# The copies out of the product with v: ScalarE's and VectorE's declared free of each other

## The chip, the cores and the metric

One core of one Trainium2 chip runs the whole kernel. The metric is the device time of one launch in microseconds (us). Below, TensorE is PE in the profile, VectorE DVE, ScalarE ACT, GpSimd POOL, and SyncE (which issues nearly all DMAs) SP.

## The reference

Attention with a threshold feeds a bilinear feed-forward layer. All data are float32.

```
q, k, v: (8 batches, 8 heads, 576 positions, 64)
s    = q @ k.T / 8                                   # 576 x 576 per head
s    = where(s >= max(s) - tau, s, -1e9)             # per row
w    = exp(s - max(s)); w = w / (sum(w) + 1e-9)
attn = w @ v
x    = attn as (8*576, 8*64) = (4608, 512)
out  = ((x @ w_a) * (x @ w_b)) @ w_out               # d_ff = 1536
```

## The kernel before

The work of the attention is cut into units. A unit is one pair of heads of one batch (32 pairs in all, `pairs`) and 128 queries; u = 4 is the remaining 64 queries of the pair. The main loop runs over the units, g counts them. One turn of it does, for unit g:

- `scores` (L335 on): TensorE multiplies q with k into two PSUM tiles `sc`, one for each head (matmuls of L347). VectorE takes the row maxima `mx` (L354) and subtracts tau, `thr` (L355).
- `weigh`: ScalarE makes the bias (L374) and the exponential `tw` (L375); VectorE compares with the threshold, multiplies and sums (L378, one operation for each head; with it the PSUM tile `sc` becomes free).
- `reciprocal` (L387 or L389, then L391 on VectorE) and `normalise` (L397 on ScalarE).
- one turn later `turn_blocks`: VectorE transposes blocks (L441), SyncE's DMAs write them to DRAM (L452) and, another turn later, read them back turned (L461, `wT`).
- three turns later (`PV_LAG`) `weighted`: the product with v. `product` fills one PSUM tile `pv` (L478), and `settle` copies it out.

`settle` is the place of the change. `pv` covers two PSUM banks, `pv[:, 0]` and `pv[:, 1]`. ScalarE copies the first bank to the left half of the target's columns (L485, `out[:, 0:n]`). VectorE copies the second bank to the right half in two operations, since its upper and lower 64 partitions trade places (L487). The target is `xT` (256 positions of a batch) or, for the last 64 positions, `xt`. When the last third of a pair's queries is done, `weighted` calls `settle` twice on the same `pv`: first columns 0 to 128 into `xT`, then 128 to 160 into `xt` (28 times in the run). The four products of the first batch's tails have `xt` alone.

The layer that records the program orders every pair of operations that touch the same tiles. So in the kernel before VectorE's copies of a `settle` wait for ScalarE's copy, and in the double call ScalarE's copy into `xt` waits for VectorE's copies into `xT`, and VectorE's copies into `xt` for that.

The first eight units (`BY_PE`) go another way: their weights are turned by TensorE (`turn_pe`, L422, copied out by ScalarE in L424 and by VectorE in L425), and `weighted_unit` calls `settle` once for each with 64 columns. In this stretch the weights of the feed-forward layer are converted too (L242, L243 on ScalarE, L249 and L268 on GpSimd, L255 and L263 on VectorE).

The feed-forward layer is a generator, `ffn`, that `advance` moves on by a number of matmul columns at several points of each turn, so that TensorE has work between the attention's steps. It multiplies the blocks `xT` and `xS` (the same with its halves of partitions exchanged, made by GpSimd in L495) with w_a and w_b into PSUM tiles `pab` (L683, and L622 in `seven_of`, which uses a scheme with seven products instead of eight), and the product of both with w_out into `po` (L728). Its PSUM tiles are emptied by ScalarE (L689, L629, L467) and VectorE (L691, L631, L638, L640, L645, L468).

All PSUM tiles (`tp`, `sc`, `pv`, `pab`, `po`) come from one pool of four slots of two banks each. A slot is given on when the last reader of its tile is done. At the end `keep_order` fixes the order of instructions on each engine as written; an engine works through its list in that order.

Of the kernel before, what the change touches and what calls it, by code (L numbers as in the profile page):

```python
# [52 lines left out]
def kernel(  # L53
# [38 lines left out]
    nc = tc.nc  # L92
    B, H, S, D = q.shape
    P = 128
# [6 lines left out]
    TAIL = S - MAIN  # L101
# [7 lines left out]
    GT = HALF // TAIL  # L109
# [16 lines left out]
    def banks(n, name):  # L126

        return psum.tile([P, 2, 512], FP32, tag="banks", name=name)[:, :, 0:n]
# [147 lines left out]
    for _ in range(TW_BUFS):  # L276
        t = work.tile([P, 2 * NB, Q], FP32, tag="tw", bufs=TW_BUFS, name="rows")
# [31 lines left out]
    x_of, xtail_of = {}, {}  # L309
# [123 lines left out]
    def width(i, h):  # L433
        return (HALF, HALF, TAIL)[h] if i < HP else (HALF, HALF + TAIL)[h]
# [35 lines left out]
    def product(wT, vm, n):  # L470

        pv = banks(n // 2, "pv")
        for s in range(NSLOT):
            for j in range(2):
                rows = slice(j * D, (j + 1) * D)
                for c in range(2):
                    y = j ^ c
                    nc.tensor.matmul(pv[c * D:(c + 1) * D, y], vm[rows, s], wT[y](rows, s),  # L478
                                     start=(s == 0), stop=(s == NSLOT - 1))
        return pv  # L480

    def settle(out, pv, c0, c1):

        n = c1 - c0
        nc.scalar.copy(out[:, 0:n], pv[:, 0, c0:c1])  # L485
        for c in range(2):
            nc.vector.tensor_copy(out[c * D:(c + 1) * D, n:2 * n], pv[(1 - c) * D:(2 - c) * D, 1, c0:c1])  # L487

    def x_tile(name):
        return work.tile([P, HP, HALF], FP32, tag="xT", bufs=XT_BUFS, name=name)  # L490

    def exchange(x, xs, hp, c0, c1, engine):

        for r in range(2):
            engine.tensor_copy(xs[r * D:(r + 1) * D, hp, c0:c1], x[(1 - r) * D:(2 - r) * D, hp, c0:c1])  # L495
# [17 lines left out]
    def weighted_unit(i, u):  # L513

        b, hp = pairs[i]
        wT = turned.pop((i, u, "pe"))
        pv = product([lambda rows, s, t=t: t[rows, s] for t in wT], loaded[i]["v"], P)
        if (b, 0) not in x_of:
            x_of[b, 0] = x_tile("xT")
            state["xs"] = x_tile("xS")  # L520
        settle(x_of[b, 0][:, hp, u * P:(u + 1) * P], pv, 0, D)
        exchange(x_of[b, 0], state["xs"], hp, u * P, (u + 1) * P, nc.gpsimd)
        if hp == HP - 1:
            state["rows"] = u + 1
            if u == 0:
                blocks.append(((x_of[b, 0], state["xs"]), ("first", b, 0)))

    def weighted(i, h):

        b, hp = pairs[i]  # L530
        n = width(i, h)
        if h < 2:
            groups = G + (n > HALF)
            wT = [turned.pop((i, 2 * h + y))[:, 0:groups] for y in range(2)]
        else:
            t = turned.pop((i, NT))
            wT = [t[:, y:y + 1] for y in range(2)]
        pv = product([lambda rows, s, t=t: t[rows, :, s] for t in wT], loaded[i]["v"], n)
        if h < 2:
            if hp == 0:  # L540
                x_of[b, h] = x_tile("xT")
            settle(x_of[b, h][:, hp, :], pv, 0, P)
            if hp == HP - 1:
                complete.append((x_of.pop((b, h)), ("half", b, h)))
        if n % HALF:
            t = b % GT
            if hp == 0 and t == 0:
                xtail_of[b // GT] = x_tile("xt")
            settle(xtail_of[b // GT][:, hp, t * TAIL:(t + 1) * TAIL], pv, (n - TAIL) // 2, n // 2)
            del loaded[i], prepared[i]  # L550
            if hp == HP - 1 and t == GT - 1:
                complete.append((xtail_of.pop(b // GT), ("tail", b - t, 0)))
# [319 lines left out]
    n = 0  # L872
# [4 lines left out]
    for g in range(len(units) + PV_LAG):  # L877
# [4 lines left out]
        if here:  # L882
            i, u = units[g]
# [6 lines left out]
        if 2 <= g < BY_PE + 2:  # L890
            weighted_unit(*units[g - 2])
            running["owed"] -= NSLOT * P // 2
# [23 lines left out]
        if g > BY_PE:  # L916
            advance(PORTIONS[1] * pace)
            n = g - PV_LAG
            if BY_PE <= n < len(units) and part(*units[n]):
                make_room()  # L920
                weighted(*part(*units[n]))
                running["owed"] -= NSLOT * width(*part(*units[n])) // 2
            if BY_PE + 1 < g <= len(units) + 1:
                turn_back(*units[g - 2])
# [78 lines left out]
```

## Time and profile before

| what | value |
|---|---|
| median of 3 runs | 1473.59 us (1470.5 to 1475.08) |
| the profiled execution's own time | 1469.17 us |
| its span in the profile | 1467.4 us |
| granted TensorE clock, mean | 0.996 |
| TensorE busy | 1404.0 us (96% of the span) |
| VectorE busy | 1020.5 us (70%) |
| ScalarE busy | 678.8 us (46%) |
| GpSimd busy | 490.4 us (33%) |
| copies of L485 (ScalarE) | 100: 68 into xT, 32 into xt |
| copies of L487 (VectorE) | 200: 136 into xT, 64 into xt |
| a copy of L485, 128x128 and 128x32 | 0.267 us and 0.186 us |
| a copy of L487, 64x128 and 64x32 | 0.285 us and 0.188 us |

A line of the waits reads: who waited <- what ended the wait: total us, how often, longest. A line of the timeline reads: start, us, engine, source line, operation, what it writes<-what it reads, how often merged into this line, and in square brackets the idle time of the engine just before and what ended it. The times are those of one execution. A matmul's end is modelled, not recorded.

### The profile page before, as it was taken

The page shows a single profiled execution, that of the slowest core. Times are in us where ns is not written, and L with a number is a line of the kernel's source. Part 1 is how long each engine was busy: PE and PEld are TensorE (multiplying, and loading weights), DVE is VectorE, ACT ScalarE, POOL GpSimd, SP SyncE. Part 2 cuts the span into 40 slices and gives each one's busy share as a digit, 9 for nine tenths or more (in the row PEclk, how much of TensorE's full clock was granted, in tenths as well). Part 3 has the DMA queues.
Part 4 walks back from the last instruction along what each step waited for, and adds up shares of the span by engine and source line. Part 5 has one row for each costly group of instructions (what it writes and reads, how often), then busy time and mean ns, then how long its engine had stood idle before and what let it go on. Part 6 is the DMA issues. An engine that isn't in the chain of part 4 may idle for free.

```text
span 1467.4 us, 70219 instructions
## 1 busy us (share of the span) xinstructions
PE 1404.0 (96%) x31136; PEld 1224.5 (83%) x31136; DVE 1020.5 (70%) x2295; ACT 678.8 (46%) x1259; POOL 490.4 (33%) x678
## 2 busy tenths in 40 slices
PE   5779999999999999999999999999999999999998
PEld 4667687788978788899889978789898879989998
DVE  6888687778776877776757777677767786644314
ACT  5877455445544554544444545344544454331011
POOL 2764703333161606042425233241516060605000
PEclk9999999999999999999999999999999999999999
DMA  9977677678656775767545866377746776450000
GB/s 206 217 198 209 159 178 193 170 165 205 176 142 160 183 199 139 178 158 174 138 129 126 193 166 162 101 165 187 184 126 153 173 180 169 120 138 17 3 17 17
DMA packets 325056, 222.82 MB, mean 152 GB/s; under 512 B 169616, under 2 KB 308880, under 8 KB 324752
## 3 DMA queue, kind: packets, MB, share of 16 engines
q1 hardware_dynamic: 322384, 217.73, 60.1%
q8 instruction: 245, 4.01, 1.2%
q10 hardware_dynamic: 2368, 0.59, 0.2%
q14 instruction: 59, 0.48, 0.1%
HBM read 128.58 MB, written 89.65 MB: 149 GB/s over the span
## 4 chain that ended last, share of the span: by engine, by line
PE 81%; DVE 9%; DMA 4%; issue 2%; ACT 2%; SPq 1%; POOL 1%; DVEq 0%; ACTq 0%
PE pab L683 33%; PE po L728 18%; PE pab L622 11%; PE pv L478 9%; PE sc L347 9%; DVE mx L354 2%; DMA wT<-swap 2%; DVE tw L441 1%; DVE tw L378 1%; SPq L452 1%; PE po L774 1%; DVE low L255 1%; DVE xT L487 0%; POOL h L697 0%; POOL xU L502 0%
## 5 line engine op out<-in xcount | busy, mean ns | idle before, releaser
L397 ACT ACTIVATE tw<-tw,rcp 128x576 f32<-128x576 f32 x272 | 197.8, 769 | 221.9 <-DVE rcp L391 221.9
L354 DVE TENSOR_REDUCE mx<-sc 128x1 f32<-128x576 f32 x288 | 205.2, 749 | 106.2 <-PE sc L347 104.5
L375 ACT ACTIVATE tw<-sc,bias,scalars 128x576 f32<-128x576 f32 x288 | 239.7, 832 | 9.9 <-ACT bias L374 0.2
L378 DVE SCALAR_TENSOR_TENSOR tw<-sc,thr,tw 128x576 f32<-128x576 f32 x288 | 224.2, 800 | 14.1 <-ACT tw L375 13.0
L728 PE MATMUL po<-wo_sb,h 64*64 64x256 f32 x3264 | 217.0, 377 | 5.3 <-DVE t L640 5.2
L588 POOL TENSOR_TENSOR t<-u,t 128x512 f32<-128x512 f32 x14 | 17.8, 1275 | 542.1 <-ACT t L629 502.0
L441 DVE STREAM_TRANSPOSE tw<-tw 128x576 f32<-128x576 f32 x272 | 196.0, 754 | 0.8 <-ACT tw L397 0.8
L347 PE MATMUL sc<-kT,qT 64*64 64x288 f32 x2016 | 188.1, 404 | 2.4 <-DVE tw L378 1.5
L478 PE MATMUL pv<-wT,vm 64*64 64x160 f32 (+3 forms) x5184 | 183.6, 273 | 6.4 <-DMA wT<-swap 3.5
L728 PEld LDWEIGHTS po<-wo_sb,h 64*64 64x64 f32 x3264 | 159.1, 133 | 34.8 <-DVE t L640 6.4
L683 PE MATMUL pab<-xS,wa_sb 64*64 64x256 f32 (+1 forms) x2560 | 177.3, 366 | 1.8 <-issue 1.8
L478 PEld LDWEIGHTS pv<-wT,vm 64*64 64x64 f32 x5184 | 164.7, 134 | 17.0 <-issue 7.3
L683 PE MATMUL pab<-xS,wb_sb 64*64 64x256 f32 (+1 forms) x2560 | 176.2, 366 | 0.9 <-issue 0.9
L697 POOL TENSOR_TENSOR h<-h 128x256 f32<-128x256 f32 x168 | 117.7, 736 | 165.7 <-PE po L728 162.2
L683 PE MATMUL pab<-xT,wa_sb 64*64 64x256 f32 (+1 forms) x2304 | 156.1, 366 | 6.1 <-ACT wo_sb L242 1.8
L728 PE MATMUL po<-sums_u,h 64*64 64x256 f32 x2448 | 158.5, 376 | 0.6 <-DVE h L645 0.6
L683 PE MATMUL pab<-xT,wb_sb 64*64 64x256 f32 (+1 forms) x2304 | 156.9, 365 | 1.6 <-DVE h L691 1.0
L683 PEld LDWEIGHTS pab<-xS,wa_sb 64*64 64x64 f32 x2560 | 130.5, 133 | 18.9 <-issue 2.2
L683 PEld LDWEIGHTS pab<-xS,wb_sb 64*64 64x64 f32 x2560 | 131.1, 133 | 16.5 <-issue 1.6
L728 PEld LDWEIGHTS po<-sums_u,h 64*64 64x64 f32 x2448 | 118.2, 133 | 22.8 <-DVE h L645 1.0
L347 PEld LDWEIGHTS sc<-kT,qT 64*64 64x64 f32 x2016 | 111.2, 133 | 28.7 <-issue 6.3
L683 PEld LDWEIGHTS pab<-xT,wa_sb 64*64 64x64 f32 x2304 | 114.8, 134 | 22.1 <-ACT wo_sb L242 2.0
(119 smaller groups left out, 2003.8 us busy)
## 6 DMA issues: line engine op xcount, KB each, us to landing
swap<-tw SPq DMA_DIRECT2D x480, 144.0 KB, 2.6
wT<-swap SPq DMA_DIRECT2D x120, 576.0 KB, 4.5
vm<-in_v_dram SPq DMA_DIRECT2D x128, 72.0 KB, 3.1
swap<-tw SPq DMA_DIRECT2D x128, 72.0 KB, 1.8
kT<-in_k_dram SPq DMA_DIRECT2D x112, 72.0 KB, 4.3
wT<-swap SPq DMA_DIRECT2D x56, 144.0 KB, 2.6
out_dram<-kept SPq DMA_DIRECT2D x30, 256.0 KB, 4.0
raw<-in_moe_w_a_dram SPq DMA_DIRECT2D x18, 256.0 KB, 6.6
```

The lines of the kernel that those rows point to most:

```text
L347: nc.tensor.matmul(sc[j if u < NT else 0][to, c], qT[r, q0:q0 + D], kT[r, c * SH:(c + 1) * SH], start=True, stop=True)
L354: nc.vector.tensor_reduce(mx[:, c], sc[j], axis=AX.XY, op=ALU.max)
L375: nc.scalar.activation(wb[j], sb[j], AF.Exp, bias=bias[:, j:j + 1], scale=e_scale)
L378: nc.vector.scalar_tensor_tensor(out=wv, in0=sb[j], scalar=thr[:, j:j + 1], in1=wv, op0=ALU.is_ge, op1=ALU.mult, accum_out=sums[:, j:j + 1])
L397: nc.scalar.activation(w, w, AF.Copy, scale=rcp[:, j:j + 1])
L441: nc.vector.transpose(w, w)
L478: nc.tensor.matmul(pv[c * D:(c + 1) * D, y], vm[rows, s], wT[y](rows, s), start=(s == 0), stop=(s == NSLOT - 1))
L588: (nc.vector if state["over"] else nc.gpsimd).tensor_tensor(*a, **kw)
L622: nc.tensor.matmul(pab[c * D:(c + 1) * D, r, y * P:(y + 1) * P], w[k][rows, w0:w0 + D], moving[k][rows], start=(k == 0), stop=(k == HP - 1))
L683: nc.tensor.matmul(pab[c * D:(c + 1) * D, r], w[rows, f // n, k, fs + c * D:fs + (c + 1) * D], moving, start=(k == 0), stop=(k == H - 1))
L697: (nc.vector if state["over"] else nc.gpsimd).tensor_tensor(*a, **kw)
L728: nc.tensor.matmul(po[c * D:(c + 1) * D, r, y], ht[rows, t0:t0 + D], other[rows, f], start=(f == 0), stop=(f == NF // 2 - 1))
```

## The change

`settle` gets the list of the copies made so far from the same `pv`, by engine. Every copy of ScalarE is declared independent of every copy of VectorE, of the same call and of an earlier call on the same `pv`. No instruction is added, removed or moved in its engine's list; only what they wait for changes, and with it which of the four PSUM slots some tiles are given.

```
-    def settle(out, pv, c0, c1):
+    def settle(out, pv, c0, c1, others):

         n = c1 - c0
-        nc.scalar.copy(out[:, 0:n], pv[:, 0, c0:c1])
-        for c in range(2):
-            nc.vector.tensor_copy(out[c * D:(c + 1) * D, n:2 * n], pv[(1 - c) * D:(2 - c) * D, 1, c0:c1])
+        one = [nc.scalar.copy(out[:, 0:n], pv[:, 0, c0:c1])]
+        two = [nc.vector.tensor_copy(out[c * D:(c + 1) * D, n:2 * n], pv[(1 - c) * D:(2 - c) * D, 1, c0:c1])
+               for c in range(2)]
+        for mine, theirs in ((one, others[1] + two), (two, others[0] + one)):
+            for a in mine:
+                for b in theirs:
+                    tc.declare_no_dep(a.ins, b.ins, reason="banks of their own")
+        others[0].extend(one)
+        others[1].extend(two)
...
-        settle(x_of[b, 0][:, hp, u * P:(u + 1) * P], pv, 0, D)
+        settle(x_of[b, 0][:, hp, u * P:(u + 1) * P], pv, 0, D, ([], []))
...
+        read = [], []
         if h < 2:
             if hp == 0:
                 x_of[b, h] = x_tile("xT")
-            settle(x_of[b, h][:, hp, :], pv, 0, P)
+            settle(x_of[b, h][:, hp, :], pv, 0, P, read)
...
-            settle(xtail_of[b // GT][:, hp, t * TAIL:(t + 1) * TAIL], pv, (n - TAIL) // 2, n // 2)
+            settle(xtail_of[b // GT][:, hp, t * TAIL:(t + 1) * TAIL], pv, (n - TAIL) // 2, n // 2, read)
```

## The prediction

> **What bounds the kernel now.** I read the page's busy times and chain first, then the waits of TensorE, then those of VectorE and ScalarE, then the timeline around single settles. The page:
>
> ```profile
> PE 1404.0 (96%) x31136; PEld 1224.5 (83%) x31136; DVE 1020.5 (70%) x2295; ACT 678.8 (46%) x1259; POOL 490.4 (33%) x678
> ...
> PE 81%; DVE 9%; DMA 4%; issue 2%; ACT 2%; SPq 1%; POOL 1%; DVEq 0%; ACTq 0%
> ```
>
> TensorE is the bound. What VectorE saves counts only where TensorE waits for it. The second line, the chain that ended last, says that 9% of the span runs through VectorE, and the chain in order of time shows most of it before 125 us, where weights are converted. The waits of TensorE between 125 and 1330 us (who <- for whom: us in total, times, longest):
>
> ```profile
> PE po L728 <- DVE t L640: 5.2, 5, 1.7
> PE pv L478 <- DMA wT<-swap: 3.5, 3, 2.2
> PE pab L622 <- DVE h L691: 2.7, 3, 1.2
> PE sc L347 <- DVE tw L378: 2.3, 2, 1.5
> ...
> PE pab L622 <- DVE u L631: 1.8, 2, 1.1
> ```
>
> All rows of this view come to 22.9 us, of which VectorE's are 14.9 us in 16 waits. That is the stock from which the change can draw. The waits it aims at stand in the waits of all engines:
>
> ```profile
> DVE xT L487 <- ACT xT L485: 127.8, 58, 6.3
> ...
> ACT xt L485 <- DVE xT L487: 18.4, 28, 0.7
> ...
> DVE xt L487 <- ACT xt L485: 8.2, 30, 0.9
> ```
>
> The first row is no gain of 127.8 us: ScalarE had itself waited for the product with v (183.4 us in 65 waits), so most of it is the wait for TensorE, only put down to the copy that came last. The timeline of one double settle shows what is the copies' own:
>
> ```profile
> 323.35 0.27 ACT L485 COPY xT<-pv 128x128 f32<-128x128 f32 x1 [1.88 <-PE pv L478]
> ...
> 323.65 0.59 DVE L487 COPY xT<-pv 64x128 f32<-64x128 f32 x2 [1.46 <-ACT xT L485]
> ...
> 324.27 0.19 ACT L485 COPY xt<-pv 128x32 f32<-128x32 f32 x1 [0.66 <-DVE xT L487]
> ...
> 324.49 0.39 DVE L487 COPY xt<-pv 64x32 f32<-64x32 f32 x2 [0.25 <-ACT xt L485]
> ...
> 325.18 1.40 DVE L354 TENSOR_REDUCE mx<-sc 128x1 f32<-128x576 f32 x2
> ...
> 328.71 0.67 PE L347 MATMUL sc<-kT,qT 64*64 64x288 f32 x5 [1.45 <-DVE tw L378]
> ```
>
> ScalarE starts when pv is done, VectorE only 0.30 us later, 0.03 us after ScalarE's end; the tail is a third and fourth link. VectorE then has no idle time until L378, for which TensorE waits 1.45 us.
>
> **What the Trainium skill says.** "Trainium Architecture — The Big Picture", section Inside one NeuronCore: the engines have their own instruction streams and meet only through semaphores; so a dropped dependency lets both copies start at once. The trace agrees insofar as each copy starts some 0.03 us after the one it waited for. "PSUM — Partial Sum Buffer", section Specifications (TRN2): ScalarE and VectorE can read PSUM in parallel at full bandwidth if they don't collide in a bank. The copies use a bank each. The trace has no settle in which both copies run, but VectorE's L354 reads PSUM as fast beside ScalarE's PSUM reads as without (timeline: two take 1.41 us at 42.32 beside L485 and L375, 1.40 us at 325.18 beside neither). "VectorE: DVE Perf Modes", section The DRAIN you can't avoid: a semaphore between operations costs VectorE nothing extra; so I give the shed signals themselves no price. No run here isolates that. "SBUF — State Buffer", section Who interferes with whom: VectorE and GpSimd take a shared port by an exclusive lock. The trace agrees: `thr` (L355) takes 0.23 us alone and 0.5 to 0.6 us beside GpSimd.
>
> **The change, part by part.** Compared as built, both programs have the same instructions in the same order on all five engines; only waits and PSUM slots differ.
>
> *A single settle into xT (L487 no longer waits for L485).* VectorE starts with ScalarE: 0.267 us for the copy plus 0.03 us, 0.30 us earlier. This holds for the single settles after 125 us, but for three (185, 193 and 1200 us) where VectorE is late anyhow.
>
> *A double settle.* VectorE gains 0.30 us, and the 0.25 us gap before xt goes too: 0.55 us, 28 times. ScalarE's 0.66 us gap goes, so its L397 is bound by VectorE's reciprocal alone, and moves up by the same 0.55 us.
>
> *The first eight settles (29 to 90 us).* Here nothing is won:
>
> ```profile
> 50.82 0.60 DVE L355 TENSOR_SCALAR thr<-mx,scalars 128x2 f32<-128x2 f32 x1
> ...
> 51.24 0.20 ACT L485 COPY xT<-pv 128x64 f32<-128x64 f32 x1
> ...
> 51.47 0.46 DVE L487 COPY xT<-pv 64x64 f32<-64x64 f32 x2
> ```
>
> VectorE comes from L355 0.03 to 0.05 us before its copy; ScalarE's copy is over by then in all eight. Cost 0.
>
> *PSUM slots.* The pool now sees pv's slot come free by two engines, and in units 4 to 9 two tiles swap slots six times. Later tiles have the same predecessors under other slot names. The one swap that can hurt is the second sc of unit 4 (near 40.5 us): it takes the slot that VectorE's second L378 frees at 40.7 us instead of one that ScalarE's L424 freed at 40.2 us. That is 0.2 us of TensorE at most. VectorE doesn't read that tile before 42.3 us, so it is hidden; were VectorE not behind there, it would cost the 0.2 us.
>
> *Added waits.* TensorE waits for two engines instead of one at pv's slot, VectorE's L255 also for ScalarE. Each new one is for a copy that ends no later than the one formerly last. Bounds: 0, and 0.05 us (a semaphore instruction on TensorE's queue lasts 0.051 us) times the three that are new: 0.15 us. I take 0.
>
> *What reaches TensorE.* VectorE's 0.55 or 0.30 us dies in its first idle time afterwards (mostly 'mx L354 <- PE sc L347': 95.3 us in 66 waits). So I went through the stretches in which TensorE lost over 0.15 us, and asked whether VectorE sat idle between the last settle and the instruction that released TensorE. I measured the loss between starts, because a matmul of 256 columns is issued every 0.054 us but shown 0.377 us long, so that the idle figure hides up to 0.3 us. After double settles, without idle time between, TensorE loses 0.38 us at 286.8, 0.93 at 305.7, 1.64 at 328.7, 0.56 at 480.7, 0.67 at 505.0, 1.30 at 932.9, 1.39 at 1007.2, 1.22 at 1099.9 and 0.42 at 1170.0 (there by ScalarE, itself behind the reciprocal). Each shrinks by the smaller of loss and 0.55: 0.38 + 7 x 0.55 + 0.42 = 4.65 us. At 631.3 it waits 0.19 us for pv's own slot, which goes. At 715.0 and 854.7, after single settles with 0.09 us idle between, 2 x 0.21 = 0.42. Sum 5.2 us.
>
> What is not won: at 942.8 (1.74 us for L640), 386.9 and 272.1 VectorE idled 1.5 us or more in between; the DMA waits for wT hang on L441, which follows such an idle time. What is late next where a stall goes: the same VectorE operation, since seven of the nine losses are above or near 0.55 us; at 286.8, 480.7 and 1170.0 it is TensorE itself. A gain of TensorE stays: all later units hang on TensorE, and the tail from 1330 us is TensorE without a wait.
>
> So the profiled execution goes from 1469.17 to 1464.0 us (1.8 us around the span stay). It lies 4.4 us under the median of the runs, below even the fastest; I take the same difference from the median: 1473.6 - 5.2 = 1468.4 us.
>
> **The rivals.**
>
> *Hidden anyway.* TensorE's waits aren't VectorE's alone: with it 0.55 us earlier, a transfer, ScalarE or the next full slot holds TensorE. For it: 96% busy, and the gaps are nine in 1200 us. Against it: in the timelines of the nine the releaser ran without idle time. If half or more is absorbed, 0 to 2.6 us are won: about 1472.3 us.
>
> *A cascade.* ScalarE and VectorE free pab and po slots earlier in stalls that the view gives to "issue", and L441's DMAs go out earlier, so that waits for wT shrink too. All of VectorE's 14.9 us can't go; doubling my gain is the limit that I see: 1463 us.
>
> *Slower: the copies hurt each other.* Place: the 60 settles into xT after 125 us, where both copies would start together. If each VectorE copy grows by over 0.15 us (half of 0.30), the pair ends later than before. Doubled to 0.57 and 0.38 us, a double settle ends 0.57 + 0.38 - 0.55 = 0.40 us later; at the nine places and some four single ones that is 9 x 0.40 + 4 x 0.27 = 4.7 us: 1478 us. Against it: the L354 row above, and ScalarE's L375 with 0.83 us throughout, whatever VectorE reads.
>
> *It does nothing* can be left out: the built program waits for PE at L487.
>
> **How the numbers follow.** Forecast 0.56, hidden 0.33, cascade 0.05, slower 0.06. A measurement of this kernel tells about 0.3% (4.4 us) from no change. The forecast's own range is 3.5 to 7 us of gain, 1466.6 to 1470.1, and 0.46 of its 0.56 lie beyond 4.4 us; with the cascade, faster 0.51. Same: 0.10 + 0.33 = 0.43, and slower 0.06. VectorE's port lock with GpSimd shifts with every change of timing: L355 differs by 0.3 us a time, at nine places, either sign, about 1 us. The range reaches from 1464.5, most of the cascade left out, to 1474.0, no gain at all with a little of that.
>
> **What would show it.** The waits of L487 for L485 must be gone, L487 waiting for pv in L478 instead, and starting within 0.1 us of L485; the gap before ScalarE's xt copy too. L487 stays at 0.285 and 0.188 us; longer ones speak for the collision. TensorE's waits for VectorE after 125 us fall from 14.9 to about 10 us, most of all at L640, L378 and L631. VectorE's idle time before L354 grows. Wrong would be: those waits gone but TensorE's unchanged (hidden), or the same sum under DMA or ScalarE.

## The result and the profile after

| what | before | after |
|---|---|---|
| median of the runs | 1472.87 us (1470.5 to 1476.39, 6 runs) | 1464.95 us (1462.41 to 1467.27, 6 runs) |
| ratio, 95% interval | | 0.9944 (0.9926 to 0.9961) |
| the profiled execution's own time | 1469.17 us | 1465.3 us |
| its span | 1467.4 us | 1463.5 us |

By the ratio the change makes the kernel faster by 0.56%, 8.2 us, with 5.7 to 10.9 us inside the interval (the two medians differ by 7.9 us). The forecast was 1468.4 us; the time lies in its range, 0.45 us above the lower end. The gain is larger than the 5.2 us of the sum, which lies outside the interval, and larger than the 3.9 us by which the two profiled executions differ. TensorE's granted clock is no cause of it: its mean over the runs is 0.9960 with the change (6 runs), 0.9955 in the 35 runs of the kernel before that stand beside the first experiments, and 0.9953 in the 6 runs of the second kernel below, which has the whole gain. So two questions are open: where the rest of the gain comes from, and why the two profiles show only half of it.

In the changed file the lines after the edit have moved: ScalarE's copies are still L485, VectorE's are now L486; L622, L631, L640, L645, L683, L691, L697 and L728 are now L629, L638, L647, L652, L690, L698, L704 and L735. First the page of the changed kernel, busy times and the chain that ended last:

```profile
PE 1401.9 (96%) x31136; PEld 1209.2 (83%) x31136; DVE 1021.0 (70%) x2295; ACT 676.8 (46%) x1259; POOL 490.8 (34%) x678
...
PE 80%; DVE 8%; DMA 6%; SPq 2%; issue 2%; ACT 2%; DVEq 0%; ACTq 0%
```

No engine works less: VectorE has 1021.0 us as before it had 1020.5. What moved is when it works. The waits of all engines in the changed kernel (who <- for whom: us in total, times, longest):

```profile
ACT tw L397 <- DVE rcp L391: 218.4, 149, 4.6
...
DVE xT L486 <- PE pv L478: 117.6, 57, 6.0
DVE mx L354 <- PE sc L347: 113.8, 81, 3.8
```

The three waits of the copies for one another are gone; VectorE now waits for TensorE's pv itself. The timeline of the settle that the prediction showed at 323.35 us:

```profile
321.65 0.27 ACT L485 COPY xT<-pv 128x128 f32<-128x128 f32 x1 [1.89 <-PE pv L478]
321.65 0.59 DVE L486 COPY xT<-pv 64x128 f32<-64x128 f32 x2 [1.17 <-PE pv L478]
321.81 0.19 ACT L485 COPY xt<-pv 128x32 f32<-128x32 f32 x1
...
322.25 0.39 DVE L486 COPY xt<-pv 64x32 f32<-64x32 f32 x2
...
322.94 1.40 DVE L354 TENSOR_REDUCE mx<-sc 128x1 f32<-128x576 f32 x2
...
326.32 0.95 PE L347 MATMUL sc<-kT,qT 64*64 64x288 f32 x11 [0.76 <-DVE tw L378]
```

Both copies start together and last as long as before (0.27, 0.19, 0.59 and 0.39 us), so from pv's end to L354 there are 1.29 us instead of 1.83: 0.54 us less. TensorE's wait for L378 shrinks from 1.45 to 0.76 us. TensorE's waits between 125 and 1330 us, after:

```profile
PE pv L478 <- DMA wT<-swap: 6.6, 6, 2.0
PE po L735 <- DVE t L647: 4.4, 4, 1.7
PE pab L629 <- DVE h L698: 2.2, 3, 1.2
...
PE sc L347 <- DVE tw L378: 1.5, 2, 0.8
PE pab L629 <- DVE u L638: 1.4, 2, 0.8
```

VectorE's rows come to 11.0 us in 14 waits, from 14.9 in 16. But the first row grew from 3.5 to 6.6 us: this execution happened to wait longer for transfers. To see both apart I compared how far TensorE had come: both traces have all 31,136 matmuls, so I took for each unit the median start of its score matmuls (L347) in one trace and in the other, and from unit to unit what TensorE won or lost. This gives 160 steps for each pair of traces. A unit's matmuls are spread over some microseconds, so with another of them in place of the median a gain can move to the step before or after, and single figures by some 0.1 us.

### The profile page after: what moved, and what is told of

It is laid out like the page before. It is cut to its first block, busy times and chain, and to the rows that moved or that the text cites. A ratio compares the mean times of both kernels' runs of the same rounds, so it can differ in the third digit from the quotient of the medians.

```text
span 1463.5 us, 70223 instructions
## 1 busy us (share of the span) xinstructions
PE 1401.9 (96%) x31136; PEld 1209.2 (83%) x31136; DVE 1021.0 (70%) x2295; ACT 676.8 (46%) x1259; POOL 490.8 (34%) x678
## 4 chain that ended last, share of the span: by engine, by line
PE 80%; DVE 8%; DMA 6%; SPq 2%; issue 2%; ACT 2%; DVEq 0%; ACTq 0%
PE pab L690 30%; PE po L735 18%; PE pab L629 12%; PE pv L478 10%; PE sc L347 9%; DMA wT<-swap 4%; DVE mx L354 2%; DVE tw L441 1%; SPq L452 1%; DVE tw L378 1%; DMA kT<-in_k_dram 1%; PE po L781 1%; DMA vm<-in_v_dram 1%; DVE low L255 1%; DVE thr L355 0%
## 5 line engine op out<-in xcount | busy, mean ns | idle before, releaser
L397 ACT ACTIVATE tw<-tw,rcp 128x576 f32<-128x576 f32 x272 | 197.8, 769 | 218.4 <-DVE rcp L391 218.4
L354 DVE TENSOR_REDUCE mx<-sc 128x1 f32<-128x576 f32 x288 | 205.4, 750 | 114.9 <-PE sc L347 113.8
L378 DVE SCALAR_TENSOR_TENSOR tw<-sc,thr,tw 128x576 f32<-128x576 f32 x288 | 224.1, 800 | 14.6 <-ACT tw L375 13.7
L735 PE MATMUL po<-wo_sb,h 64*64 64x256 f32 x3264 | 218.6, 377 | 4.7 <-DVE t L647 4.4
L347 PE MATMUL sc<-kT,qT 64*64 64x288 f32 x2016 | 189.3, 403 | 1.7 <-DVE tw L378 0.8
L735 PEld LDWEIGHTS po<-wo_sb,h 64*64 64x64 f32 x3264 | 159.8, 133 | 34.5 <-DVE t L647 5.3
L690 PE MATMUL pab<-xS,wa_sb 64*64 64x256 f32 (+1 forms) x2560 | 178.0, 366 | 2.3 <-issue 2.3
L690 PE MATMUL pab<-xS,wb_sb 64*64 64x256 f32 (+1 forms) x2560 | 176.8, 366 | 0.9 <-issue 0.9
L704 POOL TENSOR_TENSOR h<-h 128x256 f32<-128x256 f32 x168 | 117.7, 736 | 167.1 <-PE po L735 163.8
L690 PE MATMUL pab<-xT,wa_sb 64*64 64x256 f32 (+1 forms) x2304 | 156.3, 365 | 5.5 <-DVE tw L378 2.9
L735 PE MATMUL po<-sums_u,h 64*64 64x256 f32 x2448 | 160.0, 376 | 0.0
L690 PE MATMUL pab<-xT,wb_sb 64*64 64x256 f32 (+1 forms) x2304 | 157.9, 365 | 1.3 <-DVE h L698 1.1
L690 PEld LDWEIGHTS pab<-xS,wa_sb 64*64 64x64 f32 x2560 | 128.7, 133 | 22.1 <-issue 2.7
L690 PEld LDWEIGHTS pab<-xS,wb_sb 64*64 64x64 f32 x2560 | 128.7, 133 | 19.7 <-issue 1.5
L735 PEld LDWEIGHTS po<-sums_u,h 64*64 64x64 f32 x2448 | 118.6, 133 | 22.8 <-DVE h L652 0.3
L347 PEld LDWEIGHTS sc<-kT,qT 64*64 64x64 f32 x2016 | 113.1, 133 | 26.8 <-issue 3.3
L690 PEld LDWEIGHTS pab<-xT,wa_sb 64*64 64x64 f32 x2304 | 112.7, 133 | 23.7 <-POOL xS L501 3.3
```

The costliest lines, as they stand in the source:

```text
L347: nc.tensor.matmul(sc[j if u < NT else 0][to, c], qT[r, q0:q0 + D], kT[r, c * SH:(c + 1) * SH], start=True, stop=True)
L354: nc.vector.tensor_reduce(mx[:, c], sc[j], axis=AX.XY, op=ALU.max)
L378: nc.vector.scalar_tensor_tensor(out=wv, in0=sb[j], scalar=thr[:, j:j + 1], in1=wv, op0=ALU.is_ge, op1=ALU.mult, accum_out=sums[:, j:j + 1])
L397: nc.scalar.activation(w, w, AF.Copy, scale=rcp[:, j:j + 1])
L690: nc.tensor.matmul(pab[c * D:(c + 1) * D, r], w[rows, f // n, k, fs + c * D:fs + (c + 1) * D], moving, start=(k == 0), stop=(k == H - 1))
L704: (nc.vector if state["over"] else nc.gpsimd).tensor_tensor(*a, **kw)
```

## The experiments

Four kernels were run beside the kernel before on one chip (its median there: 1470.86 us in 35 runs).

**Only the first eight settles freed.** Only the calls of `weighted_unit` declare the copies independent. This kernel has all the swaps of PSUM slots that the change brought.

```
-    def settle(out, pv, c0, c1, others):
+    def settle(out, pv, c0, c1, others=None):
...
+        if others is None:
+            return
         for mine, theirs in ((one, others[1] + two), (two, others[0] + one)):
...
-            settle(x_of[b, h][:, hp, :], pv, 0, P, read)
+            settle(x_of[b, h][:, hp, :], pv, 0, P)
...
-            settle(xtail_of[b // GT][:, hp, t * TAIL:(t + 1) * TAIL], pv, (n - TAIL) // 2, n // 2, read)
+            settle(xtail_of[b // GT][:, hp, t * TAIL:(t + 1) * TAIL], pv, (n - TAIL) // 2, n // 2)
```

> Only the first eight settles (64 columns) are freed; from unit 8 on the copies stay ordered as before. The six swaps of PSUM slots in units 4 to 9 come with it. Theory A (VectorE starts 0.30 or 0.55 us earlier in the later settles, and that shows where TensorE waits for VectorE): ratio to before 0.999 to 1.001, since in the first eight VectorE comes late to its copies anyway. Theory B (the start and the other PSUM slots brought the gain): ratio about 0.9945, as the whole change.

Measured: 1470.93 us, ratio 0.9996 (0.9986 to 1.0006). The start and the slots bring nothing that the interval of 1.5 us either way would show. The timeline of the changed kernel says why, as it did before:

```profile
50.86 0.61 DVE L355 TENSOR_SCALAR thr<-mx,scalars 128x2 f32<-128x2 f32 x1
...
51.33 0.18 ACT L485 COPY xT<-pv 128x64 f32<-128x64 f32 x1
51.50 0.46 DVE L486 COPY xT<-pv 64x64 f32<-64x64 f32 x2
```

VectorE still comes from L355 at 51.47 us, when ScalarE's copy is nearly over.

**Only the later settles freed.** The opposite half: `settle` as above, but only `weighted_unit` leaves the list out.

```
-        settle(x_of[b, 0][:, hp, u * P:(u + 1) * P], pv, 0, D, ([], []))
+        settle(x_of[b, 0][:, hp, u * P:(u + 1) * P], pv, 0, D)
```

> Only the settles from unit 8 on are freed; the first eight stay ordered, and no PSUM slot differs from before. Theory A: the whole gain, ratio 0.993 to 0.9965 (1462 to 1468 us). Theory B: ratio 0.999 to 1.0.

Measured: 1463.56 us, ratio 0.9945 (0.9927 to 0.9963). The whole gain is here.

**Free, but VectorE later.** The changed kernel; VectorE makes one of its two copies twice, so that it ends about as late as if it had waited.

```
-               for c in range(2)]
+               for c in (0, 1, 0)]
```

> All copies are free of each other as in the change, but VectorE repeats one of its two copies in every settle (0.285 us into xT, 0.188 us into xt), so that its queue is as late behind a settle as before: 0.285 against 0.30 us after a single one, 0.47 against 0.55 us after a double one; ScalarE stays free. Theory A (it is VectorE's time): back to before, ratio 0.998 to 1.0005. Theory C (it is the wait itself: the signal's handling, or ScalarE freed of its 0.66 us gap): the gain stays, ratio 0.9935 to 0.9965.

Measured: 1470.74 us, ratio 0.9996 (0.9983 to 1.0009). The gain is gone though no copy of one engine waits for one of the other, and TensorE waits for L378 as long as before the change:

```profile
328.40 0.95 PE L347 MATMUL sc<-kT,qT 64*64 64x288 f32 x11 [1.45 <-DVE tw L378]
```

So it is VectorE's time behind pv that counts, not the shed semaphores and not the gap on ScalarE (ScalarE's two copies run back to back here too).

**The wait made longer.** The kernel before; ScalarE makes each of its copies three times, so that VectorE waits longer.

```
-        nc.scalar.copy(out[:, 0:n], pv[:, 0, c0:c1])
+        for _ in range(3):
+            nc.scalar.copy(out[:, 0:n], pv[:, 0, c0:c1])
```

> The kernel before, with ScalarE writing its copy three times (the same data) in every settle, so that VectorE's wait grows by 0.53 us in a single and by 0.53 + 0.37 = 0.90 us in a double settle. Theory A: about 1.7 times the change's loss on top, spread the same way, and some waits that VectorE's slack still covers now come into view: 8 to 16 us slower than before, ratio 1.0055 to 1.011. Theory B or a hidden wait: within 0.2% of before.

Measured: 1496.4 us, ratio 1.016 (1.0139 to 1.018). The loss of 25.5 us is larger than expected. At the settle above TensorE's wait for L378 is

```profile
334.92 0.95 PE L347 MATMUL sc<-kT,qT 64*64 64x288 f32 x11 [2.15 <-DVE tw L378]
```

0.70 us longer. The three copies take 0.86 instead of 0.27 us into xT and 0.62 instead of 0.19 us into xt, so a single settle is 0.59 us later and a double one 1.02 us. By the comparison of TensorE's progress, 15 units lose 0.8 us or more by it, most of them 1.0 us, 15.2 us together; 27 others lose 0.3 to 0.8 us. Five of the 15 (at 432, 454, 809, 964 and 981 us) won nothing with the change. Presumably VectorE's slack there covers the old wait but not the added one; I did not follow each. So a wait has no price per piece: up to 0.55 us less was felt in 19 units, 0.59 to 1.02 us more in 42. A small part is not the wait: right behind the 2.15 us shown above, from 336.2 us on, TensorE's granted clock in this execution is one half for 3.41 us (0.51 from 336.1 to 339 us, where the kernel before has 1.00 at the same matmuls), and TensorE loses 1.65 us more.

The next three ran beside the kernel before on one chip (its median there: 1470.26 us in 40 runs). They ask whether the gain can be had once more by taking more of VectorE's work out of the same stretch.

**Reciprocal first.** In the main loop, from the ninth unit on:

```
+        if here and g >= BY_PE:
+            reciprocal(i, u, nc.scalar if converting else nc.vector)
+            normalise(i, u)
         if g > BY_PE:
             advance(PORTIONS[1] * pace)
...
-        elif here:
-            reciprocal(i, u, nc.scalar if converting else nc.vector)
-            normalise(i, u)
```

> The changed kernel, with the reciprocal (L391) and the normalisation of unit g issued ahead of the product with v and the copies of unit g-3 instead of behind them (from the ninth unit on). Theory A (what VectorE does between the end of pv and the operation that TensorE waits for sets the time): two operations of 0.15 and 0.17 us with their gaps, 0.3 to 0.4 us for each unit, leave the stretch behind the copies, so the gain of the change is had about once more: 1456 to 1463 us where the changed kernel has 1465, ratio to before 0.988 to 0.993; TensorE's waits for VectorE between 125 and 1330 us fall from 11 to 7 or 8 us. Rival (ScalarE's start sets it, since L397 of 1.44 us now stands ahead of ScalarE's own copy): pv's slot comes free later, TensorE waits at L478 or for wT, 1465 to 1475 us.

Measured: 1468.0 us, ratio 0.9983 (0.9973 to 0.9993); so some 5 us slower than the changed kernel. At the places where the change won, TensorE wins hardly more than with the change (8.1 us instead of 7.9 in the 19 units that gain with the change; the table below has them). It loses 8 us elsewhere after 125 us, in a profiled execution that was the slowest of its 22 runs (1471.29 us). One of these places, 886 to 893 us, costs 1.35 us here and 1.33 us in the kernel with both edits below, and nothing in any other kernel. Timeline of the kernel with the reciprocal first:

```profile
889.69 1.44 ACT L397 ACTIVATE tw<-tw,rcp 128x576 f32<-128x576 f32 x2 [2.48 <-DVE rcp L391]
...
891.04 0.56 ACT L467 COPY kept<-po 128x512 f32<-128x512 f32 x1
...
891.63 0.69 DVE L468 TENSOR_TENSOR kept<-kept,po 128x512 f32<-128x512 f32 x1 [1.98 <-ACT kept L467]
...
892.47 2.82 PE L735 MATMUL po<-wo_sb,h 64*64 64x256 f32 x48 [1.12 <-DVE kept L468]
```

ScalarE's L397 now stands ahead of the copy that empties po (L467), that copy comes late, VectorE waits 1.98 us for it, and TensorE waits 1.12 us for the slot. The rival had the cause right (L397 ahead), the victim was another than it named.

**All copies by ScalarE.** The changed kernel, but

```
-        two = [nc.vector.tensor_copy(out[c * D:(c + 1) * D, n:2 * n], pv[(1 - c) * D:(2 - c) * D, 1, c0:c1])
-               for c in range(2)]
+        one += [nc.scalar.copy(out[c * D:(c + 1) * D, n:2 * n], pv[(1 - c) * D:(2 - c) * D, 1, c0:c1])
+                for c in range(2)]
+        two = []
```

> The changed kernel, but ScalarE makes all three (in a double settle all six) copies of pv and VectorE none. Theory A: VectorE loses 0.57 us in a single settle and 0.96 us in a double one behind pv, more than the 0.30 and 0.55 us that the change took away; ScalarE gains about as much and had 65 waits of 6 us mean. So 1455 to 1462 us, ratio 0.986 to 0.993, and L354, L378 come earlier. Rival (ScalarE is as near to the path as VectorE, as its L397 is only held by the reciprocal): xT, L397 and L424 come later by 0.5 to 0.9 us, and TensorE waits for ScalarE instead: 1468 to 1480 us.

Measured: 1462.59 us, ratio 0.9951 (0.993 to 0.9972), not told apart from the changed kernel. VectorE's waits between 125 and 1330 us show that the time freed is not used:

```profile
DVE mx L354 <- PE sc L347: 250.9, 122, 5.6
```

With only the later settles freed this row is 105.9 us in 75 waits. Five units (at 476, 499, 928, 1002 and 1095 us) win 0.74 to 0.88 us, 0.3 to 0.5 us more than with the change, as the theory says. Most others win no more than with the change, and the unit at 1175 us has none of the 0.7 us that the change won there. The gain in the 19 units rises from 7.9 to 9.3 us only.

**Both edits.** The two edits above in one kernel.

> Both edits of the two kernels run beside it: reciprocal and normalisation ahead of the product with v, all copies of pv by ScalarE. Theory A: the gains add until TensorE's waits for VectorE are gone (11 us of them are left in the changed kernel, of which 3 or so belong to other places): 1453 to 1459 us, ratio 0.985 to 0.991. Rival: ScalarE is behind with L397 and the copies in a row, and takes VectorE's place: 1465 to 1480 us, the waits of TensorE then name ScalarE or the DMAs of wT.

Measured: 1468.17 us, ratio 0.9982 (0.9969 to 0.9994). No gain over either; TensorE's wait for L468 is there again (2.9 us in 3 waits). The theory's forecast for these three, that whatever VectorE sheds behind pv comes back as time, failed beyond the change's own size.

The last two ask what the gain around 1180 us is, which is larger than 0.55 us (before on this chip: 1471.64 us in 26 runs). In the kernel before:

```profile
1180.15 1.87 POOL L697 TENSOR_TENSOR h<-h 128x256 f32<-128x256 f32 x2 [4.88 <-PE po L728]
1180.36 1.07 DVE L645 TENSOR_TENSOR h<-u,t 128x512 f32<-128x512 f32 x1
...
1181.48 1.09 PE L728 MATMUL po<-sums_u,h 64*64 64x256 f32 x16 [0.58 <-DVE h L645]
```

and in the changed kernel:

```profile
1178.16 0.69 DVE L652 TENSOR_TENSOR h<-u,t 128x512 f32<-128x512 f32 x1
1178.33 8.71 POOL L704 TENSOR_TENSOR h<-h 128x256 f32<-128x256 f32 x12 [5.26 <-PE po L735]
```

The same operation of VectorE takes 1.07 us when GpSimd's sums began 0.21 us ahead of it, and 0.69 us when it began 0.17 us ahead of them. TensorE then has no wait.

**Short sums, before and after.** In both kernels GpSimd's sums of h take 8 of 128 columns:

```
-                    o, x1, x2 = (hs[f + k][:, :, u * P:(u + 1) * P] for k, u in (out, a, b))
+                    o, x1, x2 = (hs[f + k][:, :, u * P:u * P + 8] for k, u in (out, a, b))
```

> The kernel before, with GpSimd's sums of h (L697 h<-h, 168 operations of 0.74 us) cut to 8 of 128 columns: most of these sums are left out, only the time counts. It asks what the 0.7 to 0.8 us at 1175 to 1185 us are that the change won there beyond its 0.30 us. Lock theory: there L645 took 1.07 instead of 0.69 us only because GpSimd's L697 had begun 0.2 us ahead of it; with L697 over in 0.1 us, L645 takes 0.7 us, TensorE's wait of 0.58 us at 1181 us falls to 0.3 us or less, and this unit gains 0.3 to 0.8 us against the kernel before. Rival: L645 takes 1.07 us still, or TensorE waits as before because VectorE began late; then the unit gains nothing. Whole time: 1464 to 1473 us, as few of the 168 stand beside an operation that TensorE waits for.

> The changed kernel with the same cut (most of the sums of h are left out). Lock theory: between this and its pair the unit at 1175 to 1185 us differs by 0 to 0.3 us, where the two whole kernels differ by 0.7 to 0.8 us; the next but one, at 1192 us, where GpSimd works on xU (L502, L508) and L355 took 0.82 us, still differs by about 1.1 us. Rival: the 0.7 to 0.8 us remain. Whole time: 5 to 8 us below its pair, ratio to before 0.989 to 0.996.

Measured: 1467.04 us, ratio 0.9972 (0.9961 to 0.9982), and 1462.21 us, ratio 0.9931 (0.9905 to 0.9958). The kernel before with short sums:

```profile
1178.81 0.22 POOL L697 TENSOR_TENSOR h<-h 128x16 f32<-128x16 f32 x1 [4.86 <-PE po L728]
1179.04 0.69 DVE L645 TENSOR_TENSOR h<-u,t 128x512 f32<-128x512 f32 x1
...
1179.79 1.09 PE L728 MATMUL po<-sums_u,h 64*64 64x256 f32 x16 [0.21 <-DVE h L645]
```

L645 takes 0.69 us, TensorE's wait falls from 0.58 to 0.21 us, and the unit wins 0.37 us. Between the two kernels it differs by 0.37 us instead of 0.7 to 0.8 (0 to 0.3 was expected), so about half of the gain of this unit is the lock, the exclusion between VectorE and GpSimd that the prediction names; the other half I put down to VectorE's 0.30 us. The expectation for the unit at 1192 us failed: the two don't differ there by 1.1 us, since the kernel before with short sums wins 1.0 us by itself. There GpSimd's work on xU, which was not cut, merely falls at another moment, and L355 takes 0.35 us where it took 0.82 us before and 0.26 us after the change. No run isolates the lock at this place, but the traces show it in another way. The unit at 178 us, which wins 0.30 us, has before the change

```profile
179.94 2.37 POOL L582 TENSOR_TENSOR first_u<-first_u,wa_sb 128x1024 f32<-128x1024 f32 x1
...
180.69 1.63 DVE L355 TENSOR_SCALAR thr<-mx,scalars 128x2 f32<-128x2 f32 x1
```

and after it

```profile
178.97 2.36 POOL L589 TENSOR_TENSOR first_u<-first_u,wa_sb 128x1024 f32<-128x1024 f32 x1
...
180.02 1.33 DVE L355 TENSOR_SCALAR thr<-mx,scalars 128x2 f32<-128x2 f32 x1
```

Both times L355 (0.23 us alone) ends some 0.02 us behind GpSimd's operation. This holds throughout: of L355 and L389, 56 instances before and 57 after the change take more than 0.3 us, and every one ends 0.02 to 0.03 us after an operation of GpSimd. The 0.30 us at 178 us are therefore the lock's, and they come in the kernel with VectorE later too (1.34 us for L355, 0.29 us won).

## Why the prediction was right, and where its size was off

What TensorE won by unit, from the mean of two traces without the gain (before, only the first eight) to the mean of two with it (after, only the later ones):

| place, us | forecast | won |
|---|---|---|
| 286.8 | 0.38 | 0.37 |
| 305.7 (and 309.2) | 0.55 | 0.54 |
| 328.7 | 0.55 | 0.69 |
| 480.7 | 0.55 | 0.21 (0 and 0.42) |
| 505.0 | 0.55 | 0.28 |
| 932.9, 1007.2, 1099.9 | 3 x 0.55 | 0.53, 0.53, 0.58 |
| 1170.0 | 0.42 | 0.04 |
| 631.3 | 0.19 | 0.54 |
| 715.0, 854.7 | 0.42 | 0.02 |
| sum of these | 5.2 | 4.3 |
| 1175 to 1200 (three units) | none | 2.0 |
| six units, at 178 (the lock), 344, 360, 546, 1038 and 1122 us | none | 1.5 |
| all | 5.2 | 7.8 |

**What bounds it, and the price of a settle: right.** L486 starts with L485, 0.30 us earlier, and 0.54 us are saved in the double settle, where 0.55 was worked out. The copies do not hurt each other: the rival "slower" is out, as the copies kept 0.27 and 0.59 us side by side.

**The start, the slots, the added waits at nothing: right.** The kernel with only these measures 0.9996.

**Hidden anyway: wrong.** 4.3 of the 5.2 us that the list named did come, and five of the twelve places within 0.05 us.

**A cascade: not seen.** By its size, 8.2 us, the gain lies between the sum and this rival's 10 us. But what the rival rests on did not shrink in the two profiled executions: TensorE's waits put to "issue" between 125 and 1330 us come to 3.5 us before and 3.8 us after, those for wT to 3.5 and 6.6 us.

**The sum: too small, by two terms.** So the range held the time by its width: what was worked out is 3 us short of the measured gain. The first term is the lock with GpSimd, put at "about 1 us, either sign" and so at nothing in the sum. It was read as 0.5 to 0.6 us for L355 beside GpSimd, where the same trace has L355 with 1.63 us at 180.69 us. It weighed on the side of the gain: 0.30 us at 178 us, and a part of the 2.0 us at 1175 to 1200 us, where VectorE got ahead of GpSimd at one operation and met it at a better moment at another; how much of the 2.0 us is VectorE's own 0.30 us, the runs show for the first of the three units only (about half). The second is the search itself: five units win 0.19 to 0.28 us each that I had not listed; together 1.3 us. None of it comes in the kernel with VectorE later beyond 0.1 us, so it is VectorE's time, but I did not find the single wait for each.

The places that gave less than forecast (480.7, 505.0, 1170.0, 715.0 and 854.7) take 1.4 us off. At two of them the forecast itself came: at 480.7 us TensorE is 0.5 us ahead in both traces, and one of them gives back 0.42 us at 482.5 us; at 1170.0 us both are 0.53 us ahead, and lose 0.33 and 0.66 us again 3 us later. All three losses fall into the middle of a product, where the traces show "issue" (0.24 and 0.40 us) or no wait at all, as in the unit at 702 us below. At 505.0 us the lock took most of the rest: in both traces L389 lasts 0.39 us, in the kernel before 0.18 us, until a copy of GpSimd beside it ends; the kernel with all copies by ScalarE wins 0.79 us there. At 715.0 and 854.7 us TensorE's waits stayed (1.44 and 0.64 us before, 1.52 and 0.64 us after).

**The profiled executions differ by 3.9 us only, because of what varies between executions.** The pair "only the first eight" and "only the later ones" differs by 9.7 us in its spans, with the same 7 to 8 us at the places above. The remainder lies where the change can't reach: the start (units at 47 to 115 us, up to 4 us either way), waits for wT, 3.0 to 7.2 us in total from trace to trace, and TensorE's granted clock. The clock falls to one half for 3.41 us at a time, at other moments in every execution: at 47.0 and 53.8 us before and at 60.5 us after the change, at 18.8, 117.8 and 257.7 us with only the first eight, at 18.6 us with only the later ones. The mean of both pairs, 6.8 us, and the places' 7.8 us stand beside 8.2 us from the runs. One loss both of these traces with the gain have: 1.27 us in the unit at 702 us. Of the changed kernel:

```profile
703.29 1.20 PE L629 MATMUL pab<-xU,first_u 64*64 64x128 f32 x35 [0.61 <-issue]
```

TensorE stops in the middle of a product for nothing that the trace shows. It doesn't go with the change: the kernel before with short sums loses 0.93 us there, the changed one with short sums 0.14 us. What it is stays open.

## What to carry to other kernels

A wait between two engines is worth what the third one, the bound, waits for behind it, place by place: here 0.30 or 0.55 us at each of 60 settles became 8 us of 1473. List the places before believing the wait's total (127.8 us here), and don't expect the gain to continue: shedding as much again from VectorE gave nothing that could be told from the change's own gain, while adding a wait was paid at once. Where two engines share a lock, ask which of two operations that start within a few tenths of a microsecond will come first after the change.

## What was not expected of the hardware

- The order of two operations 0.2 us apart decides the lock between VectorE and GpSimd: 0.69 or 1.07 us for the same 128x512 operation. A VectorE operation on two columns (L355, 0.23 us alone) took up to 1.89 us, and whenever L355 or L389 took more than 0.3 us it ended 0.02 to 0.03 us after an operation of GpSimd. With GpSimd's sums cut short, VectorE's busy time fell from 1020.5 to 1005.5 us with the same instructions.
- The kernel answers unevenly: 0.30 to 0.55 us less at each settle won 8 us; 0.59 us more at a single and 1.02 us more at a double one cost 25.5 us, of which 1.65 us in the profiled execution are a stretch of half clock.
